# Attention and MLP in one kernel: loads of K and V and the bound of K one step sooner from the seventh pair on, and one order of transposes for all pairs

## The chip, the cores and the metric

The kernel runs on one core of one Trainium2 chip. The metric is the device time of one execution in microseconds. Engines are named as the profile names them: PE is TensorE (matrix products and transposes), PEld its weight loads, DVE VectorE, ACT ScalarE, POOL GpSimd, and SP is SyncE, which here only issues transfers (SPq).

## The reference

```python
def _attn_ref(q, k, v):                      # 4 batches, 8 heads, 1152 positions, 64 wide
    q_pool = q.reshape(B, H, S // 2, 2, D).mean(axis=3)
    scores = scale * np.matmul(q_pool, k.transpose(0, 1, 3, 2))
    scores = scores - np.max(scores, axis=-1, keepdims=True)
    attn = np.exp(scores)
    attn = attn / (np.sum(attn, axis=-1, keepdims=True) + 1e-09)
    return np.matmul(attn, v)

def _moe_ref(x, g_ln, w_ch1, w_ch2):         # x: 4 x 576 x 512
    xn = (x - mu) / np.sqrt(var + 1e-06) * g_ln
    return x + np.maximum(xn @ w_ch1, 0.0) @ w_ch2
```

Attention over queries that are averaged in twos, and behind it a layer norm and a two-layer perceptron on the joined heads. All data are float32.

## The kernel before

The work is cut into 16 pairs of heads (`p`, counted from 0, four to a batch), and each pair into `C` = 9 blocks of 128 rows of queries against all 1152 keys. One block is one step `i`, 144 in all, with `i = 9 p + j`. Products are made in float16: each float32 operand is split into a high and a low part, and three products stand for one. The first 36 steps (`on_pe`, the pairs of the first batch) use another form, in which TensorE turns the weights of attention itself; the change leaves their order as it was.

From step 36 on a block passes through the engines like this, each stage in one step or the next:

- TensorE forms the scores of block i+1 (`emit_s`, L390 and L398) during step i.
- VectorE takes them from PSUM with their maximum (`emit_max`, L410). ScalarE forms the exponential (`emit_exp`, L417) and its high part (`emit_hi`, L428).
- One step later the low part follows (`emit_lo`): on VectorE (L437), in the blocks j = 2, 5, 8 on GpSimd (L435). SyncE then issues the transposing transfer of both parts (L440).
- Four steps after the block, TensorE multiplies with V (`emit_pv`, L480). VectorE and ScalarE scale the result (L528, L529, L540).
- At the end of each step TensorE does one unit of the perceptron (L631 or L663), whose result ScalarE and VectorE take out of PSUM (L644, L645, L677), and one piece of preparation for the coming pair.

Copies out of PSUM are not written in place: `until` puts them on a list, and `flush` emits them in the next step, ahead of that step's exponential (or sooner, where a bank of PSUM is needed). So a preparation of step i is evacuated by ScalarE (L274 or L299) and VectorE (L271) at the start of step i+1. Each engine works through its instructions in program order.

Preparation of pair p stands around `i0 = (p - 1) * C`, the first step of pair p-1. `load` brings K (L117, and a small repeat L118) and V (L121) over SyncE's queue; there is one buffer for K (`kr`) and one for V (`vr`). `bound` (L182, on ScalarE) sums absolute values of K, Q and V, for a power of two by which each is scaled. `scales_reduce` joins them at step i0 + 3. Then six pieces (`PREPS`) turn K and Q by TensorE into the layout for the scores, one in each of the steps i0 + 4 to i0 + 9 (one later in the first batch): `prep_k` 0 and 1 are the keys of the first and the second head, `prep_k` 2 the last block of both, `prep_q` 0 to 2 the queries. `prep_k` reads `kr`, so the next load of K can only start when its last piece is done. `take_v` (GpSimd) reads `vr` at steps i0 + 5 and i0 + 7. Q is loaded (L129) 12 steps ahead of i0.

The order of emission within a step is fixed by `step`: maximum, scores of the next block, `flush`, exponential and high part, the scaling left from the step before, low part of the block before with its transposing transfer, product with V, unit and piece of preparation, and at the very end what `at` has put down for this step: loads, bounds, `take_v`.

Of the kernel before, what the change touches and what calls it, by code (L numbers as in the profile page):

```python
# [24 lines left out]
def tile_pooled_attention_moe(  # L25
# [18 lines left out]
    nc = tc.nc  # L44
# [4 lines left out]
    C = S // 128  # L49
    HP = H // 2  # L50
# [109 lines left out]
    def pool_q(p, eng):  # L160
        x = raws[p, "q"]
        eng.tensor_tensor(x[:, :, 0], x[:, :, 0], x[:, :, 1], op=ALU.add)

    def dup_q(p, eng):
        x = raws[p, "q"]
        eng.tensor_copy(x[:, :, 1], x[:, :, 0])
# [171 lines left out]
    def prep_q_first():  # L338
# [17 lines left out]
    PREPS = (  # L356
        ((prep_k, 0), (prep_k, 2), (prep_q, 0), (prep_q, 1), (prep_k, 1), (prep_q, 2)),
        ((prep_k, 0), (prep_k, 2), (prep_q, 0), (prep_k, 1), (prep_q, 2), (prep_q, 1)),
    )


# [2 lines left out]
    def on_pe(i):  # L364

        return 0 <= i < HP * C
# [445 lines left out]
    def at(i, fn, *a):  # L812
        todo.setdefault(i, []).append((fn, a))
# [3 lines left out]
    def pre(i, fn, *a):  # L817
        early.setdefault(i, []).append((fn, a))
# [3 lines left out]

    for p in range(1, NP):
        i0 = (p - 1) * C
        at(max(i0 - 1, 0), load, p, "k", nc.sync)
        at(i0, load, p, "v", nc.sync)
        at(i0 + 1, bound, p, "k")
        if p == 1:
            pre(0, behind_scales)
            pre(i0 + 1, pool_q, p, nc.gpsimd)  # L830
            at(i0 + 1, dup_q, p, nc.gpsimd)
            at(i0 + 2, bound, p, "q")
        elif on_pe(i0):
            at(i0 - 4, load_q, p, (nc.sync,))
            at(i0 - 1, lambda p=p: calm.appendleft((lambda n: pool_q(p, nc.gpsimd), 0)))
            at(i0, lambda p=p: calm.appendleft((lambda n: dup_q(p, nc.gpsimd), 0)))
            at(i0 + 2, bound, p, "q")
        else:
            early_q = not on_pe(i0 - 6)
            at(i0 - (12 if early_q else 8), load_q, p, (nc.sync,))  # L840
            at(i0 - (6 if early_q else 4), pool_q, p, nc.vector)
            at(i0 - 2, bound, p, "q")
            at(i0 - 1, dup_q, p, nc.gpsimd)
        if not on_pe(p * C):
            at(i0 + 2, bound, p, "v")
        pre(i0 + 3, scales_reduce, p, 0, 2 if on_pe(p * C) else 3)
        for n in range(2):
            if on_pe(p * C):
                at(i0 + (5, 7)[n], gate)
            at(i0 + (5, 7)[n], take_v, p, n)  # L850
        for n, (fn, u) in enumerate(PREPS[p % HP // 2]):
            late = 1 if on_pe(i0) else 0
            pre(i0 + 4 + n + late, lambda fn=fn, p=p, u=u: preps.append((fn, p, u)))

# [324 lines left out]
```

## Time and profile before

| | before |
|---|---|
| median of 3 runs | 813.52 us (812.06 to 813.91) |
| profiled execution | 813.32 us, span 811.5 us |
| granted TensorE clock | 1.000 |
| busy: PE, DVE, ACT, POOL | 96%, 74%, 67%, 42% of the span |

The span runs from the first to the last instruction; the rest of the execution's time lies around it. Busy shares are means over stages: the first batch to about 172 us, the pipeline described above to about 700 us, and then the perceptron's remaining units alone.

### The profile page before, as it was taken

The page shows a single profiled execution, that of the slowest core. Times are in us where ns is not written, and L with a number is a line of the kernel's source. Part 1 is how long each engine was busy: PE and PEld are TensorE (multiplying, and loading weights), DVE is VectorE, ACT ScalarE, POOL GpSimd, SP SyncE. Part 2 cuts the span into 40 slices and gives each one's busy share as a digit, 9 for nine tenths or more (in the row PEclk, how much of TensorE's full clock was granted, in tenths as well). Part 3 has the DMA queues.
Part 4 walks back from the last instruction along what each step waited for, and adds up shares of the span by engine and source line. Part 5 has one row for each costly group of instructions (what it writes and reads, how often), then busy time and mean ns, then how long its engine had stood idle before and what let it go on. Part 6 is the DMA issues. An engine that isn't in the chain of part 4 may idle for free.

```text
span 811.5 us, 21278 instructions
## 1 busy us (share of the span) xinstructions
PE 781.8 (96%) x8936; PEld 551.8 (68%) x8936; DVE 598.6 (74%) x1179; ACT 544.0 (67%) x789; POOL 342.5 (42%) x342
## 2 busy tenths in 40 slices
PE   8999999989989999989999999999999999999997
PEld 6788887767565656567666665767575757766764
DVE  5899999878898986898687877887786867521221
ACT  5889888777767777787677686877677776211010
POOL 2012333576999862665453535537161532300000
PEclk9999999999999999999999999999999999999999
DMA  9736545025998989896989798987979786401001
GB/s 282 241 107 219 192 135 172 2 72 109 168 181 154 179 167 201 164 213 116 202 143 220 147 212 145 186 163 144 197 135 196 131 145 121 86 1 27 14 1 27
DMA packets 276017, 115.95 MB, mean 143 GB/s; under 512 B 259280, under 2 KB 259280, under 8 KB 275920
## 3 DMA queue, kind: packets, MB, share of 16 engines
q1 hardware_dynamic: 275440, 113.63, 67.9%
q8 instruction: 70, 1.15, 0.6%
q10 hardware_dynamic: 480, 0.95, 0.4%
q14 instruction: 27, 0.22, 0.1%
HBM read 46.14 MB, written 4.72 MB: 63 GB/s over the span
## 4 chain that ended last, share of the span: by engine, by line
PE 63%; DVE 16%; ACT 7%; DMA 6%; issue 4%; SPq 2%; POOL 2%; ACTq 0%; DVEq 0%
PE psum L663 19%; PE psum L631 17%; PE psum L390 7%; PE psum L480 6%; PE psum L471 5%; DVE pe L410 5%; PE psum L447 3%; DVE hl L437 3%; DMA vr<-in_v_dram 2%; PE psum L398 2%; ACT pe L417 2%; SPq L440 2%; DMA kr<-in_k_dram 1%; DMA stage<-in_moe_w_ch_dram 1%; PE psum L321 1%
## 5 line engine op out<-in xcount | busy, mean ns | idle before, releaser
L410 DVE CUSTOM_DVE_ANT_0 pe<-psum,nought,sc 128x1152 f32<-128x1152 f32 x144 | 203.0, 1410 | 25.2 <-PE psum L197 9.7
L417 ACT ACTIVATE pe<-pe,nb 128x1152 f32<-128x1152 f32 x144 | 180.4, 1253 | 32.4 <-DVE nb L410 31.2
L663 PE MATMUL psum<-wsl,ht 128*128 128x512 f16 x864 | 196.6, 379 | 2.5 <-DVE ht L645 2.1
L631 PEld LDWEIGHTS <-wsl 128*128 128x128 f16 x1920 | 169.6, 98 | 25.3 <-issue 7.6
L631 PE MATMUL psum<-xn,wsl 128*128 128x256 f16 x1536 | 176.3, 273 | 6.6 <-DVE xb L677 3.8
L663 PEld LDWEIGHTS <-ht 128*128 128x128 f16 x864 | 81.1, 98 | 90.9 <-issue 3.1
L428 ACT ACTIVATE hl<-pe 128x1152 f16<-128x1152 f32 x108 | 125.6, 1163 | 3.4
L390 PE MATMUL psum<-kt,qt 64*128 64x512 f16 (+1 forms) x960 | 120.2, 380 | 1.0 <-ACT qt L274 0.7
L644 ACT ACTIVATE ht<-psum 128x512 f16<-128x512 f32 x72 | 42.7, 593 | 115.4 <-PE psum L631 112.2
L437 DVE SCALAR_TENSOR_TENSOR hl<-pe,hl 128x1152 f16<-128x1152 f32 x72 | 113.3, 1573 | 0.0
L480 PE MATMUL psum<-vt,pt 128*128 128x65 f16 (+2 forms) x3240 | 106.8, 193 | 0.0
L645 DVE SCALAR_TENSOR_TENSOR ht<-psum,ht 128x512 f16<-128x512 f32 x72 | 49.3, 685 | 72.3 <-ACT ht L644 72.3
L480 PEld LDWEIGHTS <-pt 128*128 128x128 f16 (+1 forms) x3240 | 98.4, 100 | 2.6 <-issue 0.2
L239 POOL TENSOR_SCALAR pe<-pe 128x1152 f32<-128x1152 f32 x36 | 41.4, 1149 | 118.8 <-ACT hl L428 118.8
L435 POOL TENSOR_TENSOR hl<-pe,hl 128x1152 f16<-128x1152 f32 x36 | 85.6, 2378 | 3.0
L471 PE MATMUL psum<-pt,vt 128*65 128x128 f32 (+1 forms) x720 | 77.4, 263 | 1.3 <-DVE kt L271 1.3
L471 PEld LDWEIGHTS psum<-pt,vt 128*65 128x65 f32 x720 | 71.5, 138 | 1.5 <-DVE kt L271 1.5
L390 PEld LDWEIGHTS <-qt 64*128 64x128 f16 (+1 forms) x960 | 31.7, 96 | 47.6 <-issue 29.5
L398 PEld LDWEIGHTS <-qt 128*128 128x128 f16 (+1 forms) x320 | 17.6, 99 | 65.8 <-issue 65.6
L677 DVE SCALAR_TENSOR_TENSOR xb<-psum,inv,xb 128x512 f32<-128x512 f32 x32 | 23.8, 744 | 36.3 <-PE psum L663 36.1
L271 DVE SCALAR_TENSOR_TENSOR qt<-psum,s,qt 128x512 f16<-128x512 f32 (+2 forms) x49 | 29.7, 606 | 28.3 <-ACT qt L274 27.9
L453 ACT COPY pt<-psum 128x512 f32<-128x512 f32 x72 | 44.2, 639 | 7.1 <-PE psum L447 6.0
(116 smaller groups left out, 939.9 us busy)
## 6 DMA issues: line engine op xcount, KB each, us to landing
stage<-in_moe_w_ch_dram SPq DMA_DIRECT2D x32, 512.0 KB, 6.2
kr<-in_k_dram SPq DMA_DIRECT2D x16, 576.0 KB, 4.7
vr<-in_v_dram SPq DMA_DIRECT2D x16, 576.0 KB, 5.0
qr<-in_q_dram SPq DMA_DIRECT2D x31, 288.0 KB, 4.8
out_dram<-xb SPq DMA_DIRECT2D x28, 128.0 KB, 3.0
pt<-hl SPq DMA_TRANSPOSE x108, 4.9
kr<-in_k_dram SPq DMA_DIRECT2D x16, 64.0 KB, 4.5
out_dram<-xb ACTq DMA_DIRECT2D x4, 128.0 KB, 2.6
```

The source lines that it names most:

```text
L390: nc.tensor.matmul(out=sp[o:o + w, c0:c0 + 512], lhsT=qt[r:r + 64, qa, q0:q0 + w], rhs=kt[r:r + 64, ka, h], start=(a == 0), stop=(a == 2),)
L410: nc.vector.tensor_tensor_reduce(out=st["pe"], in0=st["s"], in1=nought[:, 0:1].to_broadcast([128, S]), scale=pair[i // C]["sc"][:, 0:1], s ...
L417: nc.scalar.activation(out=st["pe"], in_=st["pe"], func=ACTF.Exp, scale=-1.0, bias=st["nb"])
L428: nc.scalar.activation(out=hl[:, 0], in_=st["pe"], func=ACTF.Copy, scale=2.0 ** 15)
L435: nc.gpsimd.tensor_tensor(hl[:, 1], st["pe"], hl[:, 0], op=ALU.subtract)
L437: nc.vector.scalar_tensor_tensor(hl[:, 1], st["pe"], 2.0 ** 15, hl[:, 0], op0=ALU.mult, op1=ALU.subtract)
L453: nc.scalar.copy(st["pt"][:, a:b], st["s"][:, a:b])
L471: nc.tensor.matmul(out=ps[0:65, q0:q0 + w], lhsT=vt[:, h, c], rhs=pt[:, 128 * u + q0:128 * u + q0 + w], start=(u == 0), stop=(u == C - 1),)
L480: nc.tensor.matmul(out=dst[:, 0:n], lhsT=pt[:, a + u, q0:q0 + w], rhs=vt[:, h, c, x0:x0 + n], start=(u == 0 and a == 0 and n == 65), stop= ...
L631: nc.tensor.matmul(out=ps[:, o:o + n], lhsT=wsl[:, 8 * w + cc, wa, f * 128:f * 128 + 128], rhs=xn[:, xa * KD + cc, 0:n], start=(m == 0), s ...
L645: lambda: nc.vector.scalar_tensor_tensor(lo, pv, 0.0, hi, op0=ALU.max, op1=ALU.subtract),
L663: nc.tensor.matmul(out=ps, lhsT=hv[0][:, ha, f, t * 128:t * 128 + 128], rhs=wsl[:, 8 * w + 4 + f // 2, wa, (f % 2) * DM:(f % 2) * DM + DM] ...
```

## The change

For pairs 6 to 15 the load of K moves from the end of step i0 - 1 to the end of step i0 - 2, the load of V from the end of step i0 to that of step i0 - 1, and the bound of K from the end of step i0 + 1 to that of step i0. The bound of V and the joining of the bounds stay. In pairs 5, 8, 9, 12 and 13 `prep_k` 1 and `prep_q` 1 change places, so that `prep_k` 1 is the fourth piece, as it already was in the second two pairs of each batch; pairs of the first batch and pair 4 keep their order.

```diff
     PREPS = (
         ((prep_k, 0), (prep_k, 2), (prep_q, 0), (prep_q, 1), (prep_k, 1), (prep_q, 2)),
         ((prep_k, 0), (prep_k, 2), (prep_q, 0), (prep_k, 1), (prep_q, 2), (prep_q, 1)),
+        ((prep_k, 0), (prep_k, 2), (prep_q, 0), (prep_k, 1), (prep_q, 1), (prep_q, 2)),
     )
...
     for p in range(1, NP):
         i0 = (p - 1) * C
-        at(max(i0 - 1, 0), load, p, "k", nc.sync)
-        at(i0, load, p, "v", nc.sync)
-        at(i0 + 1, bound, p, "k")
+
+        ahead = 1 if i0 > HP * C else 0
+        at(max(i0 - 1 - ahead, 0), load, p, "k", nc.sync)
+        at(i0 - ahead, load, p, "v", nc.sync)
+        at(i0 + 1 - ahead, bound, p, "k")
...
-        for n, (fn, u) in enumerate(PREPS[p % HP // 2]):
+        for n, (fn, u) in enumerate(PREPS[p % HP // 2 or (0 if on_pe(i0) else 2)]):
             late = 1 if on_pe(i0) else 0
             pre(i0 + 4 + n + late, lambda fn=fn, p=p, u=u: preps.append((fn, p, u)))
```

## Rows read from the trace of the kernel before

**Rows 1.** Busy time in two stretches of 20 us; columns named above them.

```profile
core 0: us, PE busy (x) PEld busy (x) DVE busy (x) ACT busy (x) POOL busy (x), PEclk, DMA share, GB/s
220.00:240.00 20.00, 17.97 (x238) 12.94 (x238) 17.68 (x27) 15.39 (x23) 19.58 (x12) 1.00 1.00 196
460.00:480.00 20.00, 20.00 (x257) 12.28 (x254) 15.09 (x30) 14.74 (x22) 12.25 (x9) 1.00 0.92 178
```

**Rows 2.** Groups on ACT, 200 to 700 us: busy, mean ns | idle before, releaser.

```profile
L182 ACT ACTIVATE kt<-vr 128x1152 f16<-128x1152 f32 x10 | 11.6, 1162 | 10.4 <-DMA vr<-in_v_dram 10.4
L182 ACT ACTIVATE kt<-kr 128x1152 f16<-128x1152 f32 x10 | 11.6, 1159 | 8.4 <-DMA kr<-in_k_dram 8.2
```

**Rows 3.** Waits of PE, 200 to 700 us: total, times, longest.

```profile
PE psum L398 <- ACT xb L540: 4.8, 6, 1.6
PE psum L631 <- DVE xb L677: 3.8, 4, 1.6
PE psum L631 <- DVE ht L645: 2.2, 5, 0.8
```

**Rows 4.** Timeline of SP, pairs 6, 7, 8, 10 and 14: start, us.

```profile
212.14 4.97 SPq L440 DMA_TRANSPOSE pt<-hl  x1
...
220.13 0.59 SPq L117 DMA_DIRECT2D kr<-in_k_dram  x1
...
223.64 3.06 SPq L440 DMA_TRANSPOSE pt<-hl  x1
226.74 0.58 SPq L121 DMA_DIRECT2D vr<-in_v_dram  x1
...
254.96 4.09 SPq L440 DMA_TRANSPOSE pt<-hl  x1
...
296.82 4.08 SPq L440 DMA_TRANSPOSE pt<-hl  x1
...
384.57 4.09 SPq L440 DMA_TRANSPOSE pt<-hl  x1
...
560.40 4.31 SPq L440 DMA_TRANSPOSE pt<-hl  x1
```

**Rows 5.** Line L117, ten loads of K from 200 to 700 us: issue to landing.

```profile
DMA to landing us min/median/max: 4.3/4.9/6.5
```

**Rows 6.** Timeline of ACT, pairs 6, 7, 8, 10, 14: start, us, idle before.

```profile
220.25 0.63 ACT L540 ACTIVATE xh<-psum,r 64x64 f32<-64x64 f32 x2
220.91 0.37 ACT L274 ACTIVATE qt<-psum,s 128x128 f16<-128x128 f32 x1
...
263.02 0.63 ACT L540 ACTIVATE xh<-psum,r 64x64 f32<-64x64 f32 x2
263.68 0.69 ACT L274 ACTIVATE qt<-psum,s 128x512 f16<-128x512 f32 x1
...
306.08 0.69 ACT L274 ACTIVATE qt<-psum,s 128x512 f16<-128x512 f32 x1 [0.59 <-PE psum L321]
...
392.62 0.59 ACT L592 CAST xh<-psum 128x512 f16<-128x512 f32 x1 [1.19 <-PE psum L586]
...
567.10 0.60 ACT L644 ACTIVATE ht<-psum 128x512 f16<-128x512 f32 x1 [0.68 <-PE psum L631]
```

**Rows 7.** Timeline of DVE ahead of pairs 6 and 7: start, us, idle before.

```profile
221.31 0.35 DVE L271 SCALAR_TENSOR_TENSOR qt<-psum,s,qt 128x128 f16<-128x128 f32 x1 [0.92 <-ACT qt L274]
...
233.26 0.69 DVE L645 SCALAR_TENSOR_TENSOR ht<-psum,ht 128x512 f16<-128x512 f32 x1 [1.22 <-ACT ht L644]
...
264.40 0.75 DVE L271 SCALAR_TENSOR_TENSOR qt<-psum,s,qt 128x512 f16<-128x512 f32 x1 [1.54 <-ACT qt L274]
...
275.62 0.69 DVE L645 SCALAR_TENSOR_TENSOR ht<-psum,ht 128x512 f16<-128x512 f32 x1 [0.81 <-ACT ht L644]
```

**Rows 8.** Timeline of PE, pairs 6, 8, 10, 14: start, us, idle before.

```profile
227.19 2.78 PE L631 MATMUL psum<-xn,wsl 128*128 128x256 f16 x24 [1.60 <-DVE xb L677]
...
315.56 0.30 PE L398 MATMUL psum<-kt,qt 128*64 128x128 f16 x4 [0.82 <-ACT xb L540]
...
320.96 0.27 PE L398 MATMUL psum<-kt,qt 128*128 128x128 f16 x2 [0.69 <-ACT xb L540]
...
407.10 0.27 PE L398 MATMUL psum<-kt,qt 128*128 128x128 f16 x2 [0.32 <-ACT xb L540]
...
578.37 0.30 PE L398 MATMUL psum<-kt,qt 128*64 128x128 f16 x4 [1.65 <-ACT xb L540]
```

## The prediction

> **What bounds the kernel now.** I read the trace in this order: busy time by stretch, the waits of the loop's second part, then SyncE's queue and the engines around one pair's loads. The busy time comes first because it says which engine a saved wait must reach. TensorE is busy for 20.00 of 20 us at 460 us, but for only 17.97 of 20 at 220 us, where GpSimd is at 19.58 and VectorE at 17.68 [rows 1]. So a wait saved in pairs 6 to 8 can shorten the kernel, while in the later pairs most of it would fall into time in which another engine waits for TensorE anyway. All TensorE work is fixed; the end comes sooner only by the idle time that TensorE loses.
>
> The waits that the change aims at stand in ScalarE's rows: before the bound of V it sat idle 10.4 us in ten pairs, before the bound of K 8.4 us [rows 2]. The two bounds take 1.16 us each. TensorE itself never waits for these loads; it waits for what ScalarE and VectorE do late after them: the copy L540 (4.8 us, six times), the evacuations L677 (3.8 us) and L645 (2.2 us) [rows 3]. These are the only places where the change can pay or cost.
>
> Why V is late is seen in SyncE's queue of pair 6: K's load is issued at 220.13, then comes the transpose of a block whose low part GpSimd makes, at 223.64, and only behind it V's load, at 226.74 [rows 4]. A load needs 4.3 to 6.5 us to land, median 4.9 [rows 5]. ScalarE works in order, so what stands behind the bound waits with it.
>
> **The change part by part.** *V's load* moves up one step, to before that transpose, and its bound stays where it was. The buffer is free by then (its last reader, GpSimd's second `take_v` for the pair before, is put in the step ahead), so V lands some 5 us sooner in pair 6 and ScalarE's 10.4 us go away in all pairs. It costs no instruction more. The Trainium skill, page "DMA: Bandwidth & Descriptors", section "Rules for kernel authors", asks for this: issue the transfer early and wait for it late. By that rule the time would be that of the second rival below.
>
> *K's load* also moves up one step, but so does its bound, so this pair gains no time between issue and wait. What sets the issue is SyncE: K now comes right behind the transpose that follows the next load of Q, and that transpose is held until Q has landed: 4.97, 4.09, 4.08, 4.09 and 4.31 us in pairs 6, 7, 8, 10 and 14 [rows 4]. So K is issued at 217.15, 259.1, 300.95, 388.7 and 564.75. I take 5.0 us to landing: the median is 4.9 and the slow end, 6.5, is further off than the fast one, 4.3 [rows 5].
>
> *The bound of K* is the point on which my forecast turns. The loads and bounds for pair p fall around the start of pair p-1. At its old place, the end of the second step of pair p-1, the bound stands before an exponential that has to wait for VectorE's maximum in any case. At the new place, the end of the first step, the next thing is a copy out of PSUM: L274, the last piece of the preparation of pair p-1 itself (or L644, or L592). VectorE waits for that copy before it can do its low part and the next maximum: 0.92 us ahead of pair 6, 1.54 us ahead of pair 7 [rows 7]. There is nothing in ScalarE's queue to hide 1.16 us there. The pairs by the K that is loaded, with ScalarE's free time from [rows 6]:
>
> Pair 6: ScalarE is free at 220.88; K lands at 222.15, the bound ends at 223.3, and L274 starts 2.4 us later than its 220.91. TensorE's 1.60 us wait for L677 [rows 8], which VectorE does behind this, becomes 4.0. VectorE makes good the 1.22 us that it waited for L644 behind V [rows 7], and TensorE, which soon waits for VectorE again [rows 3], ends up with it: 2.4 - 1.2 = 1.2 us lost.
>
> Pair 7: free at 263.65, K lands at 264.1, L274 starts at 265.25 for 263.68: 1.57, less the 0.81 waited for L644 [rows 7]: 0.75 lost.
>
> Pair 8: free at 305.49, but L274 waits for TensorE to 306.08, a cover of 0.59 [rows 6]. K lands at 305.95, L274 starts at 307.1: 1.0 later. But the two waits of TensorE for L540, 0.82 and 0.69 [rows 8], come from the old waits for K and V and go: 1.0 - 1.5 = 0.5 gained.
>
> Pair 10: free at 391.43, cover 1.19 before L592 [rows 6]. K lands at 393.7, L592 starts 2.25 later. TensorE feels between nothing and 2.25 of it; I take 1.0, since this pair lies where TensorE sets the pace, less the 0.32 wait [rows 8]: 0.7 lost.
>
> Pair 14: free at 566.42, cover 0.68 [rows 6]; K lands at 569.75 and L644 starts 3.85 later. The later wait of 1.65 [rows 8] goes with the old bound. Bounds: 1.65 gained if all is absorbed, 3.85 - 1.65 = 2.2 lost if none is. I take 0.5 lost, nearer to the lost side because L540, on which TensorE waits, stands behind L644.
>
> Pairs 9, 11, 12, 13 and 15: nothing. TensorE is at or near its full share there [rows 1], and what follows the bound waits for TensorE.
>
> *The order of the turning* swaps one transposition of four blocks for another in five pairs; each fills one bank and is evacuated a step later as before: nothing. It only makes K's buffer free a step sooner, which the earlier load needs; without it SyncE would wait at K's load and hold the transposes behind it. Two transposes now come later behind loads, and one sooner. I cost that at nothing, because the product that reads a block's transpose is issued four steps after the block; if loads take their worst, that cover is thin.
>
> **Sum.** 1.2 + 0.75 - 0.5 + 0.7 + 0.5 = 2.65 us. The profiled execution took 813.32 us (span 811.5 and 1.8 around it), 0.2 under the median of three, 813.52. So 813.3 + 2.7 = 816.0 us. Each tenth of a microsecond in K's landing moves five pairs, so the sum by 0.5. At 4.3 us everywhere the sum would be -0.85, 812.5; at 6.5 everywhere 10.1, 823.4; with half of the pairs that late, 819.6.
>
> **The rivals.**
> *K lands quickly, no change.* At 4.3 to 4.7 us the sum is between -0.85 and 1.15: 812.5 to 814.5. For it: the fast end of [rows 5]. Against: K's load now runs at once beside a transpose on either side.
>
> *The earlier loads pay, faster.* If the evacuation behind the new bound has the slack to wait (VectorE catches up inside the same pair, from TensorE's idle share of 220 to 240 us), only what the late loads cost TensorE counts: 0.82 + 0.69 + 0.32 + 1.65 [rows 8] is 3.5, with pairs 6 and 7 at nothing: 809.8. It decides when L274's delay, 2.4 and 1.6 us here, no longer shows up in the wait for L677. For it: 18.8 us of ScalarE's idle time are at stake [rows 2]. Against it: VectorE was waiting for just that copy [rows 7], so it has no slack at that place.
>
> *K lands late as well, much slower.* Three loads of a pair (Q, K, V) now come in consecutive steps, each stretching the transpose behind it. The Trainium skill, same page, section "Issuing engines are not separate DMA queues", says that all transfers of a core share 16 engines and interleave; a transpose behind Q's load taking 4.1 to 5.0 us [rows 4] agrees. Then 819.6 to 823.4.
>
> **Chances and range.** Slower by more than 0.2% (1.6 us, about what a measurement of this kernel can tell from no change): 0.45, of which 0.08 for the last rival. Within 0.2%: 0.28. Faster: 0.27. The range runs from 810, where the fast rival lies, to 820, where half of the K loads are late; about 0.1 is left out on either side. The likeliest case's own range is 814.5 to 819.6.
>
> **What would show it.** ScalarE's wait for V before L182 gone, against 10.4 us; its wait for K about as large as now, 7 to 10 us, but at step 0; V's load issued before GpSimd's transpose; VectorE's wait for L274 (before L271) ahead of pairs 6 and 7 at about 3.3 and 3.1 us against 0.92 and 1.54; TensorE's wait for L677 ahead of pair 6 about 4.0 us against 1.60. I am wrong if the wait for L677 has not grown, which means that the copy behind the bound had slack, or if K lands before ScalarE is free.

## The result, and the profile after

The changed kernel takes 823.96 us (median of 4 runs, 821.48 to 825.30) against 813.18 for the one before: ratio 1.0117, 95% interval 1.0097 to 1.0137. It is slower by 10.8 us; the forecast was 816.0 and its range ended at 820. From line 359 on, the changed kernel's line numbers are one higher than before's (L399 is L398 of before, L587 is L586, L632 is L631, L646 is L645), up to the lines of the change.

The profiled execution took 825.3 us, its span is 823.5, 12.0 more than before's. Of these, 2.5 us stand ahead of step 9 and do not belong to the change: there the granted clock was at half from 14.05 to 20.87 us. Up to there all kernels here have the same instructions; some of their profiled executions show such a fall (V's load alone for 3.41 us, from 14.74 on), others none (the kernel before, the order alone). The remaining 9.4 us were lost between steps 36 and 143.

The groups of ScalarE's two bounds after (columns as in [rows 2]):

```profile
L182 ACT ACTIVATE kt<-kr 128x1152 f16<-128x1152 f32 x10 | 11.6, 1164 | 6.1 <-DMA kr<-in_k_dram 5.9
L182 ACT ACTIVATE kt<-vr 128x1152 f16<-128x1152 f32 x10 | 11.5, 1152 | 0.0
```

K's landing after (as in [rows 5]):

```profile
DMA to landing us min/median/max: 4.4/4.7/5.2
```

The wait for V is gone, 10.4 to 0; that for K is 6.1 instead of 8.4, and nearly all of it stands in pairs 10 (2.27) and 14 (3.18). K lands a little sooner than the 5.0 that the sum took. So what the change aims at on ScalarE came about: 12.7 us less idle time ahead of the two bounds. TensorE's own waits after (columns as in [rows 3]):

```profile
PE psum L632 <- DVE ht L646: 5.9, 7, 3.3
PE psum L587 <- DVE qt L271: 4.0, 2, 3.5
PE psum L632 <- DVE xb L678: 3.0, 4, 1.5
PE psum L399 <- ACT xb L541: 2.7, 3, 1.0
```

Against [rows 3] the wait for L541 fell from 4.8 to 2.7 and that for L678 from 3.8 to 3.0, but the wait for L646 grew from 2.2 to 5.9, and before L587 TensorE waits 4.0 us: 0.51 in pair 9, as it did before (L586), and 3.52 in pair 10, which are new. Pair 10, timeline of the changed kernel:

```profile
392.60 0.59 SPq L117 DMA_DIRECT2D kr<-in_k_dram  x1
...
394.44 0.61 ACT L541 ACTIVATE xh<-psum,r 64x64 f32<-64x64 f32 x2
397.33 1.16 ACT L182 ACTIVATE kt<-kr 128x1152 f16<-128x1152 f32 x1 [2.27 <-DMA kr<-in_k_dram]
...
398.61 0.37 ACT L274 ACTIVATE qt<-psum,s 128x128 f16<-128x128 f32 x1
399.01 0.35 DVE L271 SCALAR_TENSOR_TENSOR qt<-psum,s,qt 128x128 f16<-128x128 f32 x1 [5.30 <-ACT qt L274]
...
399.51 0.88 PE L587 MATMUL psum<-ident,xs 128*128 128x128 f32 x4 [3.52 <-DVE qt L271]
...
400.42 0.58 ACT L593 CAST xh<-psum 128x512 f16<-128x512 f32 x1 [1.44 <-PE psum L587]
```

Read it from below: TensorE stands still 3.52 us until VectorE's L271 has emptied a bank, L271 waited 5.30 us for ScalarE's L274, and L274, which itself takes 0.37 us, stood behind the bound, which waited 2.27 us for K. Pair 14 is the same chain with another copy:

```profile
572.99 2.78 PE L632 MATMUL psum<-xn,wsl 128*128 128x256 f16 x24
...
574.51 0.63 ACT L541 ACTIVATE xh<-psum,r 64x64 f32<-64x64 f32 x2
...
576.69 0.98 PE L481 MATMUL psum<-vt,pt 128*128 128x65 f16 x27
...
578.31 1.16 ACT L182 ACTIVATE kt<-kr 128x1152 f16<-128x1152 f32 x1 [3.18 <-DMA kr<-in_k_dram]
...
579.59 0.60 ACT L645 ACTIVATE ht<-psum 128x512 f16<-128x512 f32 x1
...
580.22 0.69 DVE L646 SCALAR_TENSOR_TENSOR ht<-psum,ht 128x512 f16<-128x512 f32 x1 [5.27 <-ACT ht L645]
...
580.97 4.28 PE L632 MATMUL psum<-xn,wsl 128*128 128x256 f16 x24 [3.29 <-DVE ht L646]
```

The last row shows a second cost. The same 24 products took 2.78 us in the first row and 4.28 here: behind the stall TensorE ran at its lower clock. The windows of the changed kernel (columns as in [rows 1]):

```profile
220.00:240.00 20.00, 18.48 (x256) 12.85 (x255) 15.98 (x30) 16.03 (x22) 19.58 (x12) 1.00 1.02 194
260.00:280.00 20.00, 17.54 (x209) 10.66 (x204) 15.51 (x24) 14.86 (x21) 19.67 (x12) 0.91 1.11 213
400.00:420.00 20.00, 20.00 (x242) 13.91 (x242) 13.65 (x25) 13.65 (x18) 3.94 (x3) 0.92 0.79 147
460.00:480.00 20.00, 19.71 (x249) 12.20 (x246) 16.62 (x33) 15.11 (x21) 11.76 (x9) 1.00 0.87 151
580.00:600.00 20.00, 19.04 (x190) 10.73 (x190) 13.43 (x23) 12.33 (x17) 3.60 (x3) 0.91 0.82 154
```

The mean granted clock is 1.00 in two of them and 0.91 or 0.92 in the three that hold a fall. In each, the clock was at half (1.2 instead of 2.4 GHz) for 3.41 us, from 273.46, 399.75 and 580.66 on. So a fall costs an estimated 4.28 - 2.78 = 1.5 us. A busy share hides this: in the window at 400 us TensorE is "busy" for 20.00 of 20 us, and slow.

By pairs (us from the start of VectorE's maximum in step i0 - 4 to that in step i0 + 5, for the pair whose K is loaded; pairs 11, 12, 13 and 15 are the same before and after):

| pair | before | after | bound back | fillers, right bank | dummy | K ahead of Q |
|---|---|---|---|---|---|---|
| 6 | 43.56 | 43.64 | 43.65 | 44.12 | 43.67 | 43.71 |
| 7 | 42.78 | 44.78 | 42.85 | 43.30 | 42.98 | 42.98 |
| 8 | 42.28 | 41.38 | 41.17 | 41.51 | 41.50 | 42.20 |
| 9 | 41.66 | 41.84 | 41.49 | 41.85 | 44.26 | 42.20 |
| 10 | 44.48 | 49.17 | 44.11 | 47.89 | 45.39 | 45.39 |
| 14 | 45.06 | 48.30 | 44.05 | 47.28 | 44.48 | 45.72 |

After less before: +0.1, +2.0, -0.9, +0.2, +4.7, +3.2, together 9.3 us. The other columns are experiments told below.

### The profile page after: what moved, and what is told of

The parts are those of the page before. It is cut to its first block, busy times and chain, and to the rows that moved or that the text cites. A ratio compares the mean times of both kernels' runs of the same rounds, so it can differ in the third digit from the quotient of the medians.

```text
span 823.5 us, 21281 instructions
## 1 busy us (share of the span) xinstructions
PE 789.3 (96%) x8936; PEld 556.2 (68%) x8936; DVE 593.3 (72%) x1179; ACT 545.4 (66%) x789; POOL 341.8 (42%) x342
## 3 DMA queue, kind: packets, MB, share of 16 engines
q8 instruction: 70, 1.15, 0.6%
## 4 chain that ended last, share of the span: by engine, by line
PE 73%; DVE 15%; ACT 5%; issue 3%; DMA 3%; SPq 0%; POOL 0%; DVEq 0%; ACTq 0%; POOLq 0%
PE psum L632 20%; PE psum L664 20%; PE psum L391 8%; PE psum L481 8%; PE psum L472 5%; DVE pe L411 5%; PE psum L448 3%; DMA kr<-in_k_dram 3%; DVE hl L438 3%; PE psum L399 2%; PE psum L321 1%; DVE ht L646 1%; ACT pe L418 1%; PE psum L1079 1%; DVE kt L271 1%
## 5 line engine op out<-in xcount | busy, mean ns | idle before, releaser
L411 DVE CUSTOM_DVE_ANT_0 pe<-psum,nought,sc 128x1152 f32<-128x1152 f32 x144 | 203.1, 1411 | 34.8 <-PE psum L197 18.8
L632 PEld LDWEIGHTS <-wsl 128*128 128x128 f16 x1920 | 171.0, 98 | 29.8 <-issue 10.5
L632 PE MATMUL psum<-xn,wsl 128*128 128x256 f16 x1536 | 179.3, 275 | 9.3 <-DVE ht L646 6.2
L645 ACT ACTIVATE ht<-psum 128x512 f16<-128x512 f32 x72 | 42.9, 596 | 125.5 <-PE psum L632 122.3
L438 DVE SCALAR_TENSOR_TENSOR hl<-pe,hl 128x1152 f16<-128x1152 f32 x72 | 110.6, 1536 | 0.0
L646 DVE SCALAR_TENSOR_TENSOR ht<-psum,ht 128x512 f16<-128x512 f32 x72 | 49.3, 685 | 67.7 <-ACT ht L645 67.6
L399 PEld LDWEIGHTS <-qt 128*128 128x128 f16 (+1 forms) x320 | 17.3, 99 | 64.7 <-issue 64.4
L271 DVE SCALAR_TENSOR_TENSOR qt<-psum,s,qt 128x512 f16<-128x512 f32 (+2 forms) x49 | 29.7, 606 | 38.1 <-ACT qt L274 37.6
L678 DVE SCALAR_TENSOR_TENSOR xb<-psum,inv,xb 128x512 f32<-128x512 f32 x32 | 23.8, 744 | 36.7 <-PE psum L664 36.7
```

The costliest lines, as they stand in the source:

```text
L411: nc.vector.tensor_tensor_reduce(out=st["pe"], in0=st["s"], in1=nought[:, 0:1].to_broadcast([128, S]), scale=pair[i // C]["sc"][:, 0:1], s ...
L438: nc.vector.scalar_tensor_tensor(hl[:, 1], st["pe"], 2.0 ** 15, hl[:, 0], op0=ALU.mult, op1=ALU.subtract)
L632: nc.tensor.matmul(out=ps[:, o:o + n], lhsT=wsl[:, 8 * w + cc, wa, f * 128:f * 128 + 128], rhs=xn[:, xa * KD + cc, 0:n], start=(m == 0), s ...
L646: lambda: nc.vector.scalar_tensor_tensor(lo, pv, 0.0, hi, op0=ALU.max, op1=ALU.subtract),
```

## The experiments

**Theory A**: the cost lies in the new place of the bound of K, ahead of ScalarE's copies out of PSUM, and the earlier loads by themselves pay a little. **Rival B**: the earlier loads hold up SyncE's transposes. **Rival C**: the order in which keys and queries are turned. Four runs take the change apart. Each was timed in several rounds beside the kernel before, whose median was 813.61 us.

*V's load alone* (kernel before):

```diff
-        at(i0, load, p, "v", nc.sync)
+        at(i0 - (1 if i0 > HP * C else 0), load, p, "v", nc.sync)
```

> The kernel before with the load of V alone one step sooner in pairs 6 to 15. Theory A (the cost is the bound of K in front of ScalarE's copies out of PSUM): this part is harmless, the 10.4 us of ScalarE's wait for V go, the waits of TensorE behind V (0.69 in pair 8, 0.9 in pair 9, 0.3 in pair 10) go: 810 to 812.5 us, clock 1.00 throughout. Rival B (the earlier loads are the cost, since they hold the transposing transfers back): TensorE waits for pt and the time is 815 us or more.

Measured: 812.07 us, ratio 0.9982 (0.9971 to 0.9994). V's part alone makes the kernel faster, by 0.2%.

*The bound back in its old place* (changed kernel):

```diff
-        at(i0 + 1 - ahead, bound, p, "k")
+        at(i0 + 1, bound, p, "k")
```

> The changed kernel with the bound of K alone put back to the end of step i0 + 1; both loads stay one step sooner, the order of the pieces stays changed. Theory A: ScalarE waits for neither K nor V (under 1 us in all), the TensorE waits of 3.52 and 3.29 us ahead of pairs 10 and 14 are gone, and so are the falls of the clock; also 0.82, 0.69 and 1.65 of before go: 807.5 to 811 us. Rival B: the loads are as early as in the changed kernel, so 819 us or more. Rival C (the order of the pieces): 819 us or more.

Measured: 812.32 us, ratio 0.9987 (0.9976 to 0.9998). One line takes back the whole slowdown, so B and C fall as its cause. ScalarE's two groups in this kernel:

```profile
L182 ACT ACTIVATE kt<-vr 128x1152 f16<-128x1152 f32 x10 | 11.5, 1153 | 0.0
L182 ACT ACTIVATE kt<-kr 128x1152 f16<-128x1152 f32 x10 | 11.5, 1152 | 0.0
```

All 18.8 us of waits [rows 2] are gone, and yet the kernel gains little, less than A expected: 1.3 us by the medians, 2.5 by the pairs of the two traces (table), of which pair 8 gives 1.1 and pair 14 1.0. Single traces differ by about half of that: with the order alone, where nothing is loaded sooner, pairs 10 and 14 are 0.4 and 0.8 us shorter than before too. TensorE's waits (columns as in [rows 3]) show where the rest went:

```profile
PE psum L632 <- DVE ht L646: 3.2, 6, 1.0
PE psum L632 <- DVE xb L678: 2.4, 4, 1.0
PE psum L481 <- DMA pt<-hl: 1.8, 4, 0.5
PE psum L399 <- ACT xb L541: 0.7, 1, 0.7
```

The waits for L541 and L678 are 5.5 us less than before, but that for L646 is 1.0 more, and 1.8 us for transposes are new: a small part of B is there, covered by what the loads save. Most of ScalarE's waiting had cost TensorE nothing.

*K's part alone* (changed kernel, V loaded as before):

```diff
-        at(i0 - ahead, load, p, "v", nc.sync)
+        at(i0, load, p, "v", nc.sync)
```

> The changed kernel with the load of V put back to the end of step i0; K's load and bound and the order of the pieces stay changed. Theory A: the long TensorE waits ahead of pairs 10 and 14 and the falls of the clock stay, and ScalarE's waits for V are back: 820 to 827 us. Rival B: V's transfer no longer collides, the time is about half way, 816 to 819 us.

Measured: 821.99 us, ratio 1.0105 (1.0084 to 1.0126). The cost goes with K. In this trace L587 waits 3.31 us in pair 10 and the clock falls behind it and in pair 14, but not in pair 7, where the stalls are much the same (1.12 and 1.33 us here, 0.94 and 1.51 in the changed kernel); pair 7 takes 43.28 here and 44.78 there, 1.5 us apart.

*The order alone* (changed kernel with nothing loaded or bounded sooner):

```diff
-        ahead = 1 if i0 > HP * C else 0
+        ahead = 0
```

> The changed kernel with loads and bound all at their old places; only the order of the six pieces is changed in five pairs. Theories A and B: 812.4 to 814 us, no different from before. Rival C: 3 us or more of the cost are here, 816 us or more.

Measured: 812.64 us, ratio 0.9995 (0.9984 to 1.0006): nothing, as forecast.

Four more runs ask what it is about the place: the copies behind it, the wait, the clock. A, B and C are from here on the ones that each expectation names. Before's median beside them was 812.81 us.

*TensorE kept busy in its stalls* (changed kernel, with small products that nobody reads):

```diff
+        if p == 10:
+            at(i0, lambda: fill_pe(54))
...
+            if i in (56, 118):
+                fill_pe(24 if i == 56 else 50)
             some_units(i)
...
+    def fill_pe(n):
+        for _ in range(n):
+            nc.tensor.matmul(
+                out=psum[:, 2, 388:512], lhsT=ident16, rhs=ident16[:, 0:124], start=True, stop=True
+            )
```

> The changed kernel with 54, 50 and 24 small matrix products of TensorE that nobody reads, put in its order just ahead of the instructions that stand still in pairs 10, 14 and 7 (3.52, 3.29 and 1.51 us of idle time in the changed kernel). They take no wait away, they only keep TensorE busy in it. Theory A: the stalls themselves cost about 5 us, and the fall of the granted clock to half for 3.41 us behind each of the three costs some 1.4 us more apiece; with TensorE busy the clock stays at 1.0 there and about 4 us come back: 819 to 820.5, and the 24 products of the unit behind pair 14's stall take 2.8 us and not 4.28. Rival B, the falls cost nothing because other engines set the pace there: 822.5 to 825. Rival C, the products come in the way of the work behind them: above 825.

Measured: 830.71 us, ratio 1.0212 (1.0192 to 1.0232), in the range of its rival C, the products come in the way. In pairs 7 and 14 the fillers write a bank that L541 has yet to empty, and wait for it with the whole queue of TensorE behind them. The row of pair 14:

```profile
583.78 5.22 PE L1082 MATMUL psum<-ident 128*128 128x124 f16 x50 [5.31 <-ACT xb L541]
```

Only pair 10 tells something: its fillers ran, its clock stayed up, and it took 47.89 us instead of 49.17.

*The bound behind the copies* (changed kernel):

```diff
-        at(i0 + 1 - ahead, bound, p, "k")
+        if ahead:
+            mid[i0 + 1] = p
+        else:
+            at(i0 + 1, bound, p, "k")
...
             flush()
+            if i in mid:
+                bound(mid[i], "k")
             if live:
                 emit_exp(i)
```

> The changed kernel with the bound of K one place later in ScalarE's order: not at the end of step i0, but in step i0 + 1, behind the copies out of PSUM and ahead of the exponential. K is loaded as early as in the changed kernel and the bound still waits for it. Theory A, it is the copies behind the bound that cost the time: almost all of it comes back, 812 to 814. Rival B, ScalarE loses the same wait and the exponential comes as late, so that the cost stays: 818 to 824.

Measured: 812.30 us, ratio 0.9990 (0.9979 to 1.0001). As expected by A: a few places later in ScalarE's order, behind `flush`, the bound costs nothing, though ScalarE still waits 1.5 us for K in pair 14.

*K's load on GpSimd's queue* (changed kernel):

```diff
-        at(max(i0 - 1 - ahead, 0), load, p, "k", nc.sync)
+        at(max(i0 - 1 - ahead, 0), load, p, "k", nc.gpsimd if ahead else nc.sync)
```

> The changed kernel with the load of K issued by GpSimd's queue instead of SyncE's, so that it no longer stands behind the transpose that SyncE holds for the load of Q; the bound stays in its new place ahead of the copies. K should then land before ScalarE is free in pairs 10 and 14, where the waits for K are 2.27 and 3.18 us. Theory A, the place costs only where the bound waits there: pairs 10 and 14 give back most of 4.7 and 3.2 us, pair 7 (wait 0.24) keeps its 2.0: 815 to 818. Rival B, the 1.2 us of the bound itself ahead of the copies are enough: 820 to 823. Rival C, a load on GpSimd's queue disturbs GpSimd's own work or the transposes: above 823.

Measured: 822.25 us, ratio 1.0125 (1.0091 to 1.0159). The number lies in the range of B, but the run does not speak for it, since the wait that it was to remove grew: issued there, K takes 6.8 us to land in the median, up to 12.1, and ScalarE waits 12.6 us for it instead of 5.9. The Trainium skill, page "DMA: Bandwidth & Descriptors", section "Issuing engine by pattern", calls transfers from the sync and scalar queues generally faster than those from GpSimd; 4.7 against 6.8 us agrees. The cost went where the wait went: pair 14, now without a wait, takes 44.12 us, and pair 9, with one of 7.84, takes 50.10 instead of 41.84. (The trace is of the slowest of the six executions, 830.05 us.)

*The bound back in pairs 10 and 14 alone* (changed kernel):

```diff
-        at(i0 + 1 - ahead, bound, p, "k")
+        at(i0 + 1 - (0 if p in (10, 14) else ahead), bound, p, "k")
```

> The changed kernel with the bound of K back in its old place in pairs 10 and 14 alone. Theory A, the cost is local, 4.7 us in pair 10, 3.2 in pair 14 and 2.0 in pair 7: 7.9 us come back, 815 to 817. Rival B, the cost is a sum of small delays in all ten pairs that pass on from pair to pair: two of ten pairs give back 2 us, 821 to 822.5.

Measured: 813.62 us, ratio 1.0011 (0.9997 to 1.0025). Two of ten pairs hold the whole loss that can be measured; more came back than A said, because with the bound back pair 14 also drops before's wait of 1.65 us [rows 8] (one of 0.98 for a transpose came in its place), and because pair 7 kept its clock in this trace (43.27 us).

The last four settle sizes. Before's median beside them was 812.93 us.

*The fillers in the right bank*: as above, but `fill_pe(50, 5)` and `fill_pe(24, 5)` write the bank that TensorE has just written itself.

> The same 54, 50 and 24 small products as in the run with fillers before, but those of pairs 14 and 7 write the bank of PSUM that TensorE has just written itself, so that they need not wait for ScalarE's copy L541 out of the other bank. Theory A, the falls of the clock cost some 1.3 to 1.5 us each (pair 10 gave back 1.28 us in the run before, where its fillers did run): no stretch at half clock in pairs 7, 10 and 14, and 820 to 822 against 824. Rival B, the falls cost nothing: 823 to 825.

Measured: 819.14 us, ratio 1.0066 (1.0050 to 1.0082): 4.8 us less than the changed kernel and below A's range, with 128 matrix products more; no stretch at half clock is left. Pair 14 in this trace, and its window:

```profile
573.18 2.87 PE L1082 MATMUL psum<-ident 128*128 128x124 f16 x50
574.46 1.16 ACT L182 ACTIVATE kt<-kr 128x1152 f16<-128x1152 f32 x1 [3.65 <-DMA kr<-in_k_dram]
...
577.11 2.78 PE L632 MATMUL psum<-xn,wsl 128*128 128x256 f16 x24 [1.06 <-DVE ht L646]
```

```profile
572.00:592.00 20.00, 18.94 (x252) 12.40 (x249) 11.53 (x22) 12.96 (x18) 3.60 (x3) 1.00 1.08 183
```

ScalarE waits for K even longer than in the changed kernel (3.65 against 3.18), the stall of TensorE's real work is longer, 2.87 + 1.06 for 3.29, and yet the 24 products behind it take 2.78 us. B falls. The 4.8 us are not the price of the three falls alone, though: the changed kernel's trace also holds the fall at 14.05 us (2.5 us), which this one has not. Between steps 36 and 143 this trace is 2.7 us shorter: pairs 7, 10 and 14 give back 1.5, 1.3 and 1.0 (table), pair 14 with a stall that is 0.64 longer, which agrees with some 1.5 us for a fall. Pairs 6 and 11, which hold no filler, take 0.5 us more each; why is open.

*ScalarE busy without a wait* (changed kernel; the real bound is in its old place, and a second activation over weights stands in the new one):

```diff
-        at(i0 + 1 - ahead, bound, p, "k")
+        at(i0 + 1, bound, p, "k")
+        if ahead:
+            at(i0, dummy, p)
...
+    def dummy(p):
+        junk = kt_of(p).rearrange("p a h n -> p (a h n)")[:, 0:S]
+        src = wsl[:, 0:2].rearrange("p m a n -> p (m a n)").bitcast(FP32)[:, 0:S]
+        nc.scalar.activation(
+            out=junk, in_=src, func=ACTF.Abs, accum_out=pair[p]["acc"][:, 0:1]
+        )
```

> The changed kernel with the bound of K back in its old place, and in the new place a second activation of the same shape that reads weights which have long been there: ScalarE's 1.2 us stand ahead of the copies in all ten pairs, without a wait for K. Theory A, the wait for K is what costs: pair 7 loses about 0.5, the others nothing, 812 to 814.5. Rival B, any 1.2 us ahead of the copies cost as much as the bound did: 818 to 824.

Measured: 816.24 us, ratio 1.0032 (1.0020 to 1.0043), between the two theories: against the same kernel without the dummy (ratio 0.9987) 1.2 us of work ahead of the copies in each of ten pairs cost 0.45%, 3.7 us in all. The bound itself, with its wait for K, costs 1.30% against the same kernel (1.0117), 10.6 us; so about a third of the loss is there without any wait for K, and the rest comes with the wait. In pair 10 the chain is the one of the changed kernel with a shorter stall:

```profile
393.03 1.16 ACT L814 ACTIVATE kt<-wsl 128x1152 f16<-128x1152 f32 x1
...
394.31 0.37 ACT L274 ACTIVATE qt<-psum,s 128x128 f16<-128x128 f32 x1
394.71 0.35 DVE L271 SCALAR_TENSOR_TENSOR qt<-psum,s,qt 128x128 f16<-128x128 f32 x1 [3.05 <-ACT qt L274]
...
395.21 0.63 PE L587 MATMUL psum<-ident,xs 128*128 128x128 f32 x4 [1.27 <-DVE qt L271]
```

The other place is pair 9: TensorE waits 2.00 us for L541 at 357.42 and the clock falls from 357.29 on, 2.8 us more than with the bound back.

*K ahead of Q in SyncE's queue* (changed kernel; nothing but SyncE's order changes):

```diff
-            at(i0 - (12 if early_q else 8), load_q, p, (nc.sync,))
+            at(i0 - ((11 if i0 > HP * C + C else 12) if early_q else 8), load_q, p, (nc.sync,))
```

> The changed kernel with the load of Q for the pair after one step later, behind the load of K in SyncE's queue, so that K no longer stands behind the transpose that is held for Q. Nothing changes on ScalarE, VectorE, GpSimd or TensorE; the bound stays ahead of the copies. Theory A, K lands some 4 us sooner, ScalarE's waits of 2.27 and 3.18 us in pairs 10 and 14 go, and with them most of their 4.7 and 3.2 us: 813 to 816. Rival B, the place costs also without a wait: 820 to 824. Rival C, the transpose that is now held for Q is a later one that TensorE needs: a wait of TensorE for pt appears, and the time stays above 817.

Measured: 816.17 us, ratio 1.0032 (1.0020 to 1.0045), just above the range of A and below those of B and C. The wait for K is 0.02 in pair 10, where the stall is 1.27 us and the pair takes 45.39, exactly as with the dummy; in pair 14 it is still 1.96. C has a small part: TensorE waits four times for transposes, 3.2 us together, against 0.3 in the changed kernel.

*K's load not sooner* (changed kernel):

```diff
-        at(max(i0 - 1 - ahead, 0), load, p, "k", nc.sync)
+        at(max(i0 - 1, 0), load, p, "k", nc.sync)
```

> The changed kernel with the load of K left where it was before, and its bound in the new place: the wait for K ahead of the copies becomes some 4 us longer in every pair (K landed 3.5 to 7.6 us after ScalarE's last work at that place in the trace of before). Theory A, each microsecond of wait ahead of the copies that exceeds what TensorE has in store is lost in full, and a long one costs 1.5 us more by the clock: 845 to 865. Rival B, the wait is mostly absorbed: 825 to 835.

Measured: 860.69 us, ratio 1.0575 (1.0554 to 1.0596), in A's range. ScalarE's wait in the new place is now 38.1 us:

```profile
L182 ACT ACTIVATE kt<-kr 128x1152 f16<-128x1152 f32 x10 | 11.6, 1162 | 38.1 <-DMA kr<-in_k_dram 38.1
```

The kernel lost 47.8 us against before, and TensorE's clock was at half for 37.6 us in six stretches between steps 36 and 143. Its trace lost 45.9 us between these steps; the clock can have cost at most half of its 37.6, 18.8, so at least 27 are not the clock's. With the clock, a microsecond of wait in front of the copies costs a microsecond and more here.

No version here beats the kernel before by much: V's load alone, at 0.9982, is the best.

## Why the prediction was wrong

The direction was right, and so was the place of the cost: ScalarE's copies behind the bound of K. The size was 8 us short, and two steps failed. The chain behind the bound in pair 10 was taken too short (0.7 us forecast, 4.7 measured), and the fall of TensorE's clock behind long stalls had no term (some 4.5 of the 9.4 us lost in the loop). Ahead of both stood the reading that TensorE's waits in [rows 3] are "the only places where the change can pay or cost": the largest new wait, 3.52 us before L587, came where pair 10 had none. By its steps:

*V's load*: right, 10.4 us of ScalarE's time and nothing lost. *The order*: right, nothing. *Pairs 9, 11, 12, 13 and 15*: nothing, right (0.2 in pair 9, 0 in the others). *The loads' effect on transposes*: nothing, right for this change (TensorE waits once, 0.3 us, for a transpose); with the bound back it is 1.8.

*Pair 14, when things happen*: right almost to the tenth. In before's time (subtract the 8.7 us lost until there, L541 at 574.51 for L540 at 565.79) ScalarE was free at 566.4, as forecast, K landed at 569.6 for 569.75 (with 4.7 us to landing, where the sum took 5.0), and the copy behind the bound started at 570.9 for 570.95. *What it costs*: wrong. I wrote "I take 0.5 lost", with an upper bound of 2.2. Measured is 3.2: the stall of 3.29 less the 1.65 that went, which is 1.6 and inside the bounds, and some 1.5 for the clock.

*Pair 10*: the step that failed most. Its "free at 391.43, cover 1.19 before L592" took the bound to stand behind L274 and ahead of L592. Before, this place looked like this:

```profile
390.42 0.61 ACT L540 ACTIVATE xh<-psum,r 64x64 f32<-64x64 f32 x2
391.06 0.37 ACT L274 ACTIVATE qt<-psum,s 128x128 f16<-128x128 f32 x1
...
391.46 0.35 DVE L271 SCALAR_TENSOR_TENSOR qt<-psum,s,qt 128x128 f16<-128x128 f32 x1 [1.77 <-ACT qt L274]
...
391.96 0.63 PE L586 MATMUL psum<-ident,xs 128*128 128x128 f32 x4
```

In the order written out, the bound is put down for the end of the step ahead of the transposes of the norm (L587), and it is these that call for a bank and so bring out L274. So three copies and TensorE's transposes stood behind the bound one after the other: L593 came 3.8 us later than before, not 2.25, and TensorE felt 3.52 of it directly, where I had allowed "between nothing and 2.25". With the clock: 3.52 less 0.32 of before's wait plus some 1.5 is 4.7, the measured sum; I had 0.7. The times of issue and landing were right here as well (K 393.3 for 393.7 in before's time, 4.0 us less by the starts of L540 above and of L541 at 394.44).

*Pair 7*: 0.75 forecast, 0.5 measured where the clock stayed up (43.28 and 43.27 against 42.78) and 2.0 where it fell.

*Pair 6*: 1.2 forecast, 0.1 measured. VectorE's wait for L274 was 2.43 and not 3.3, and VectorE made up more than the 1.2 that I allowed. Before:

```profile
221.58 3.25 DVE L437 SCALAR_TENSOR_TENSOR hl<-pe,hl 128x1152 f16<-128x1152 f32 x1
```

After:

```profile
225.46 0.35 DVE L271 SCALAR_TENSOR_TENSOR qt<-psum,s,qt 128x128 f16<-128x128 f32 x1 [2.43 <-ACT qt L274]
225.72 1.75 DVE L438 SCALAR_TENSOR_TENSOR hl<-pe,hl 128x1152 f16<-128x1152 f32 x1
```

The low part behind the copy took 1.75 us instead of 3.25, which gives back 1.5; why it is shorter there is not shown. TensorE's wait for L678 did not grow to 4.0, it became 0.73, with 0.79 for L541 ahead of it. So my own sign for "the copy had slack", that this wait has not grown, held for pair 6 and not for pairs 10 and 14. *Pair 8*: 0.5 gain forecast, 0.9 measured.

*What had no term*: the clock. The sum moved waits about and priced each at its own length. By the estimate of 1.5 us a fall, some 4.5 of the 9.4 us lost in the loop are TensorE running at 1.2 GHz after it had stood still. The fillers in the right bank, which left no fall, brought the kernel to 819.14 us, inside the range that ended at 820. The Trainium skill, page "TensorE: Matmul & The Clock Gate", section "Why this matters for your kernels", asks for no long idle gaps of TensorE between products, or its clock halves; the stalls of 3.52 and 3.29 us with a fall within 0.4 us of the end of each agree, while the falls at shorter stalls (0.94 and 1.51 us in pair 7, 2.00 us in the run with the dummy) go beyond it. A forecast that lets a wait of TensorE grow from 1.65 [rows 8], behind which the clock stayed up, to twice that has to price this.

*The rivals*: "the earlier loads pay, faster" was right about the loads and wrong about the whole. With the bound left in its place they do pay, but about 1.3 us and not 3.5: the price was read from TensorE's waits for L540, but when these went, others (for transposes, and for L646) came in their place. The Trainium skill's rule (page "DMA: Bandwidth & Descriptors", section "Rules for kernel authors"), issue early and wait late, agrees with the runs once it is read in full: the change issued K early, and waited for it early too. "K lands late as well" gave 819.6 to 823.4, near the measured time, for a reason that did not occur: no landing took over 5.2 us; with the median as measured, 4.7, the prediction's own sum gives 1.15 us, further off than its 2.65. (Its 819.6 for half of the pairs late is 819.7 by its own terms, which changes nothing.)

What stays open is why pair 7's clock fell in the changed kernel's trace and not in others with stalls of the same length, and the price of a fall is an estimate from pairs 7, 10 and 14.

## What to carry to other kernels

Moving a wait on an engine that works in order moves everything behind it: before pricing a move, write down the instructions that follow in the emitted order, copies that a bank's reuse pulls forward among them, and who waits for each. When a stall reaches TensorE, add the price of the slow stretch behind it (some 1.5 us here, nearly half of the loss), and look at the granted clock and at the duration of equal instructions, since busy shares don't show it. Here the loads could be started earlier at no net cost; what waits for a load belongs behind the copies that free PSUM, not in front of them.

## What was not expected of the hardware

Within 1 us of the end of stalls of TensorE of 3.52, 3.31, 3.29 and 2.85 us (pairs 10 and 14 of the changed kernel and of K's part alone) the granted clock fell to half for 3.41 us, all four times; at one of 2.00 us (pair 9 with the dummy) it did as well, at one of 2.08 us (pair 14 with K ahead of Q) it did not. Small products in the stall, 2.87 us of them with 1.06 us idle behind, kept it at full speed. But two shorter stalls, 0.94 and 1.51 us one after the other, did it too in the changed kernel (fall at 273.46), and so did 1.01 and 1.36 us with K on GpSimd's queue (273.75), while 1.12 and 1.33 us at the same place in K's part alone did not: the length of a stall alone does not tell these cases apart. A load of K issued by GpSimd took 6.8 us to land in the median and up to 12.1, against 4.7 and 5.2 from SyncE.
